# Ninth MLP tile: three groups of row blocks in seven half-size products instead of two, and w1's sums made two tiles sooner

## The chip, the cores and the metric

The kernel runs on one core of a Trainium2 chip. The metric is the device time of one execution in microseconds (us). Before the change three runs gave 312.92 us (median), 311.91 us and 319.43 us; the execution that was profiled took 311.71 us.

TensorE (PE in the profile) multiplies, with its weight loads on a row of their own (PEld). VectorE (DVE), ScalarE (ACT) and GpSimd (POOL) do the element-wise work, and SyncE (SP) issues transfers. Each engine runs its own instructions in the order in which they stand, and waits where an operand that another engine makes is not ready, or where a buffer that it writes is still being read.

## The reference

Attention with decays for 8 batches, 8 heads, 576 positions and head size 64 gives `x`, of 8 x 576 rows with 512 columns. A low-rank mixer over the positions follows, and then an MLP with a first layer `w_ch1` (512 to 2048) and a second layer `w_ch2` (2048 to 512):

```python
xt = x.transpose(0, 2, 1)
h = xt @ U @ V
u = x + h.transpose(0, 2, 1)
ch = np.maximum(u @ w_ch1, 0.0) @ w_ch2
return (u + ch).astype(np.float32)
```

## The kernel before, in words

The 4608 rows of `u` are cut into nine MLP tiles of 512 rows, `j` = 0 to 8; the text counts them from one, so that the ninth tile is `j` = 8. `u` transposed lies in `uT_t`. While tile `j` is in the MLP, the attention of batch `j + 1` is woven into it; batch 7, the last, belongs to the seventh tile (`j` = 6). The eighth and ninth tiles have no attention beside them and are written out in `last_tiles`.

**First layer of a tile.** Its 2048 outputs are 16 row blocks of 128. A plain block ("M" in the lists below, `unit(n)` for n below 16) is four matmuls of 128x512 into one PSUM bank, then a relu on ACT into `y1_t` (`y_t` in the profile). The blocks come in the order 0, 8, 1, 9, 2, 10 and so on. Group g is blocks 2g, 2g + 1, 8 + 2g and 9 + 2g, that is, four blocks: group 0 is M 0 to M 3, and group 3 is M 12 to M 15.

**A group in seven products.** Instead of four plain blocks, a group can be computed by Winograd's form of Strassen's product: seven products of half the rows, half the depth and half the blocks, of four matmuls of 128x256 each. The text writes "7/0" for product 7 of group 0. `seventh(n, g)` does this, with three PSUM banks for a group:

- bank a, from the pool `ps_mm` of three banks: 1, then 6, 7 and 4 are added to it in turn. After 1, 6 and 7 ACT copies the bank to an SBUF buffer `kept` (the rows `COPY q_all<-ps_y`), and the next of the chain may write only once the copy has read. After 4 ACT writes the relu.
- bank c, from the pool `one`: 5, and later 3.
- bank d: half of a tile of two banks from the pool `two`, taken once for each MLP tile; group g takes half g % 2.

After 2, after the later of 5 and 7, and after 3, DVE adds a copy to a bank and takes the maximum with zero (`finish`: a TENSOR_TENSOR `y_t<-ps_y,q_all` and a TENSOR_SCALAR `y_t<-y_t`). The copies lie in `shares[g % 2]`, the two query buffers `q_all0` and `q_all1`. `sum_up(a, z)` then makes two sums of a group's outputs for the second layer on DVE (`y_sums`).

The products need sums of quarters of `w1` (`sum_of_w1`, four tiles in the freed key and value buffers: `w1_sums` is `k_all2`, `v_all2`, `k_all0`, `v_all0`) and of the tile's `uT_t` (`sum_of_u`, four in `v_all1` for the eighth tile and `k_all1` for the ninth). Both are made on DVE.

**Second layer.** In the tiles from the third on it is also seven products, each of two units of 16 matmuls of 128x256 (units 16 to 29; `NF` is 16), on banks a, b and c of `ps_mm`. DVE drains them (`o_sb<-ps_y,o_sb`), POOL adds `u` to three of the partial results (`o_sb<-o_sb,u_t`), and SP stores.

**Order.** Everything is emitted in one program order, which each engine keeps. In tiles two to seven a list of steps with a place (a unit's number, fractions too) is merged with the units; in `last_tiles` the order was written out in loops. Before the change both last tiles take groups 1 and 2 in seven products and groups 0 and 3 in plain blocks, and the sums of `w1`, over blocks 2 to 5 of each half (1024 elements a row of a partition), are made at the start of the eighth tile, between that tile's sums of `u`.

Of the kernel before, what the change touches and what calls it, by code (L numbers as in the profile page):

```python
# [67 lines left out]
def kernel(  # L68
# [18 lines left out]
    B, H, S, D = q.shape  # L87
# [8 lines left out]
    NF = dff // P  # L96
# [5 lines left out]
    NT = B * S // 512  # L102
# [191 lines left out]
    def scale_head(b, h):  # L294

        x = v_sets[b % NSET][:, :, h, :]
        act.activation(out=x, in_=x, func=AF.Copy, scale=vs64[:, h:h + 1])


    def clear_pads(b):  # L300
        m, pad = (NB - 1, slice(HALF, P)) if b % 2 == 0 else (0, slice(0, HALF))
        for x in (k_sets, v_sets):
            pool.memset(x[b % NSET][pad, m, :, :], 0.0)

    def load_for_turns(b):

        for c in range(0, NB, 2):
            pair = range(c, min(c + 2, NB))
            load_q(b, pair)
            for m in pair:  # L310
                load_block(k_sets[b % NSET], k, b, m)
        for m in range(NB):
            load_block(v_sets[b % NSET], v, b, m)
# [13 lines left out]
    def wait_for_turns(b):  # L327

        wanted = [ch % NRING for ch in range(4 * b, 4 * b + 4)]
        for a, n in turns_of(b):  # L330
            if any(ch in wanted for ch in range(a, a + n)):
                pool.tensor_copy(out=landed[:, 0:n], in_=ring["uT"][:, a:a + n, 0, 0])
# [250 lines left out]
    def attention_steps(b, at, gap, at_mixer, at_turn=2):  # L583

        x_t = work.tile([P, NB, dm], BF16, tag="x_t", name="x_t")
        sts = [{} for _ in range(NHP)]
        mst = {}
        steps = []

        for hp in range(NHP):  # L590
            if b < NRUNS:
                steps.append((at[hp] - (3 if hp else 1), 4, lambda hp=hp: scale_v(b, hp)))
            steps.append((at[hp], 1, lambda hp=hp: att_transposes(b, hp, sts[hp])))
            steps.append((at[hp] + gap, 2, lambda hp=hp: visit(b, hp, sts, x_t)))
        steps.append((at[NHP], 0, lambda: visit(b, NHP, sts, x_t)))
        steps.append((at_mixer, 0, lambda: mix_middle(b, x_t, mst)))
        steps.append((at_mixer + 2, 0, lambda: mix_up_full(b, x_t, mst)))
        part = (NB - 1) * (1 - b % 2)
        steps.append((at_mixer + (2.5 if b % 2 else 5 if b > 2 else 8), 0, lambda: (
            mix_up(b, part, x_t, mst))))  # L600
        for i, (a, n) in enumerate(turns_of(b)):
            steps.append((at_mixer + 3.2 + i, 1, lambda a=a, n=n: mix_turn_by_dma(a, n)))
        if NTURN <= b + 1 < B:
            for i, (src, dst, c) in enumerate(
                    (src, dst, c) for c in range(0, NB, 2)
                    for src, dst in ((in_blocks(q_raw[(b + 1) % NQ]), qT_sets[(b + 1 - NTURN) % 2]),
                                     (k_sets[(b + 1) % NSET], kT_sets[(b + 1 - NTURN) % 2]))):
                steps.append((at_turn + i, 5, lambda src=src, dst=dst, c=c: (
                    turn_by_dma(src, dst, c))))
        steps.sort(key=lambda s: s[:2])  # L610
        return steps
# [324 lines left out]
    def w1_quarter(i, c):  # L936
        return w1_sb[:, 2 * c:2 * c + 2, i * HF * P:(i + 1) * HF * P]

    def sum_of_w1(n, a, z):

        f = slice(a * P, z * P)
        (a11, a12), (a21, a22) = ([w1_quarter(i, c)[:, :, f] for c in range(2)] for i in range(2))
        s1, s2, s3, s4 = (x[:, :, f] for x in w1_sums)
        to, x, y, op = (
            (s1, a21, a22, ALU.add), (s2, s1, a11, ALU.subtract),
            (s3, a11, a21, ALU.subtract), (s4, a12, s2, ALU.subtract),
        )[n]
        dve.tensor_tensor(out=to, in0=x, in1=y, op=op)

    def sums_of_w2(part):  # L950

        f = slice(part * HF // 2, (part + 1) * HF // 2)
        (b11, b12), (b21, b22) = (
            [w2_sb[:, fh * HF:(fh + 1) * HF, q * HD:(q + 1) * HD][:, f, :] for q in range(2)]
            for fh in range(2)
        )
        t3, t2, t4 = (w2_sums[:, i, f, :] for i in range(3))
        for to, x, y, op in (
            (t3, b22, b12, ALU.subtract), (t2, t3, b11, ALU.add), (t4, b21, t2, ALU.subtract),
        ):  # L960
            dve.tensor_tensor(out=to, in0=x, in1=y, op=op)

    def last_sum_of_w2(part):
        f = slice(part * HF // 2, (part + 1) * HF // 2)
        x = w2_sb[:, 0:HF, HD:dm][:, f, :]
        dve.tensor_tensor(out=x, in0=x, in1=w2_sb[:, 0:HF, 0:HD][:, f, :], op=ALU.subtract)
# [406 lines left out]
    n = 16  # L1373
# [79 lines left out]
            tc.tile_pool(name="ps_" + name, bufs=n, space=bass.MemoryType.PSUM))  # L1453


    def last_tiles():

        tiles = [mlp_units(j) for j in (NT - 2, NT - 1)]
        for i in range(4):
            steps = [lambda: tiles[0][1]["sum_of_u"](i), lambda: sum_of_w1(i, 2, 6)]  # L1460
            for step in steps if i < 2 else steps[::-1]:
                step()
        for units, steps in tiles:
            seventh, sum_up = steps["seventh"], steps["sum_up"]
            for n in range(3):
                units[n]()
            seventh(1, 1)
            units[3]()
            for n, g in ((6, 1), (2, 1), (5, 1), (7, 1)):
                seventh(n, g)  # L1470
            sum_up(0, 2)
            for n, g in ((1, 2), (2, 2), (4, 1), (6, 2), (5, 2), (3, 1), (7, 2)):
                seventh(n, g)
            sum_up(2, 4)
            for n, x in zip(range(12, NF), (4, 3, None, None)):
                units[n]()
                if x:
                    seventh(x, 2)
                if x == 3:
                    sum_up(4, 6)  # L1480
            for n in range(NF, NF + 14):
                units[n]()
                if n == NF + 11 and steps is tiles[0][1]:
                    for i in range(4):
                        tiles[1][1]["sum_of_u"](i)

    for j in range(1, NT - 2):
        if j == 1:
            clear_pads(4)
        steps = []  # L1490
        if j == 1:
            steps = sorted(
                attention_steps(2, (5, 8.5, 12, 15.5, 21), 1.5, 22, 8) + late
                + [(at, 3, lambda i=i: sums_of_w2(i)) for i, at in enumerate((3.2, 21.5))],
                key=lambda s: s[:2]
            )
        elif j + 1 < B:
            last = 17 if j < 5 else 16
            steps = attention_steps(j + 1, (-1.5, 2.5, 6.5, 10.5, last), 1.5, last + 1.8)
        if j == 2:  # L1500
            steps += [(at, 3, lambda i=i: last_sum_of_w2(i)) for i, at in enumerate((2, 3))]
        if 1 < j and j + 2 < B:
            wait_for_turns(j)
            load_for_turns(j + 2)
            if j + 3 < B:
                clear_pads(j + 3)
        if j + 2 < B:
            at = 22 if j == 1 else 20
            steps += [(at + h, 4, lambda h=h: scale_head(j + 2, h)) for h in range(H)]
        steps.sort(key=lambda s: s[:2])  # L1510
        for n, unit in enumerate(units1 if j == 1 else mlp_units(j)[0]):
            while steps and steps[0][0] <= n:
                steps.pop(0)[2]()
            if j > 1 or n >= 3:
                unit()
        for s in steps:
            s[2]()
    last_tiles()


# [29 lines left out]
```

## Time and profile before

| | |
|---|---|
| median of three runs | 312.92 us (311.91 to 319.43) |
| the profiled execution | 311.71 us |
| its span, first to last instruction | 310.0 us |
| PE busy | 302.9 us, 98% of the span |
| DVE busy | 244.7 us, 79% |
| ACT busy | 165.9 us, 54% |
| POOL busy | 131.8 us, 43% |
| granted TensorE clock | 1.00 throughout |
| eighth tile's first layer begins on PE at | 255.76 us |
| ninth tile's first layer begins on PE at | 281.05 us |
| ninth tile's second layer begins on PE at | 294.10 us |

Times within the span are counted from the span's start. A row of the timeline gives start, length, engine, operation, the tile written and those read, the shape, the count, and in brackets how long the engine was idle before and who ended that. A row with a count above one runs together instructions that follow each other. The length of such a row reaches a little into the next row, since instructions overlap; the distance between starts is what an instruction takes of its engine.

### The profile page before, as it was taken

How to read it: one execution, taken by the hardware profiler on the slowest of the kernel's cores; microseconds unless marked ns; L12 is line 12 of the kernel's file. 1: busy time of each engine (PE TensorE's matmuls, PEld its weight loads, DVE VectorE, ACT ScalarE, POOL GpSimd, SP SyncE). 2: the span in 40 equal slices, each digit the busy share in tenths (PEclk: the TensorE clock that was granted, in tenths of full speed). 3: DMA queues.
4: the chain of work that ended last, by engine and by line, in shares of the span. 5: the costliest groups of instructions: out<-in, count | busy, mean ns of one | idle time of the engine just before them, and what ended most of it. 6: DMA issues, size and time to landing. Idle time of an engine off the chain costs nothing.

```text
span 310.0 us, 9604 instructions
## 1 busy us (share of the span) xinstructions
PE 302.9 (98%) x4000; PEld 193.8 (63%) x4000; DVE 244.7 (79%) x598; ACT 165.9 (54%) x346; POOL 131.8 (43%) x172
## 2 busy tenths in 40 slices
PE   8899999999999999999999999999999999999995
PEld 3664446645544557845784578457855786686684
DVE  6867818878988997899689968996789788954954
ACT  8657605357625774567447844674377506504610
POOL 8592249649302952495158615940300030040040
PEclk9999999999999999999999999999999999999999
DMA  7999999999995999799999999999920043003003
GB/s 119 198 198 200 204 208 158 174 166 140 159 154 144 154 148 136 102 182 157 141 162 182 132 129 152 194 149 134 183 69 4 3 92 128 2 29 109 0 2 136
DMA packets 154523, 40.58 MB, mean 131 GB/s; under 512 B 139088, under 2 KB 153456, under 8 KB 154480
## 3 DMA queue, kind: packets, MB, share of 16 engines
q0 software_dynamic: 91344, 17.09, 72.2%
q1 hardware_dynamic: 63136, 22.88, 42.2%
q8 instruction: 31, 0.51, 0.7%
q14 instruction: 12, 0.10, 0.1%
HBM read 36.85 MB, written 9.44 MB: 149 GB/s over the span
## 4 chain that ended last, share of the span: by engine, by line
PE 85%; DMA 6%; DVE 5%; issue 1%; POOL 1%; SPq 0%; DVEq 0%
PE ps_y L25 70%; PE xh L25 5%; PE ps_b L25 4%; DMA kv_runs<-in_k_dram 2%; DMA kv_runs<-in_v_dram 2%; DMA y_sums<-in_k_dram 2%; PE sc L25 2%; PE ps_h L25 1%; PE pss L25 1%; DVE v_all L25 1%; PE ps_at L25 1%; DVE V_sb L25 1%; PE psq L25 0%; DVE qT_all L25 0%; DVE q_all L25 0%
## 5 line engine op out<-in xcount | busy, mean ns | idle before, releaser
L25 PE MATMUL ps_y<-uT_t,w_sb 128*128 128x512 bf16 (+1 forms) x544 | 121.6, 373 | 0.1
L25 ACT ACTIVATE y_t<-ps_y 128x512 bf16<-128x512 f32 x132 | 78.4, 597 | 57.4 <-PE ps_y L25 55.7
L25 PEld LDWEIGHTS <-w_sb 128*128 128x128 bf16 x560 | 52.9, 98 | 53.7 <-issue 0.4
L25 POOL TENSOR_TENSOR o_sb<-o_sb,u_t 128x512 f32<-128x512 f32 x21 | 23.9, 1151 | 106.5 <-DVE o_sb L25 99.2
L25 PEld LDWEIGHTS <-y_t 128*128 128x128 bf16 x576 | 55.1, 98 | 18.9
L25 PE MATMUL ps_y<-w_sb,y_t 128*128 128x256 bf16 (+1 forms) x352 | 57.5, 312 | 0.0
L25 DVE SCALAR_TENSOR_TENSOR S<-S,keep,pss 128x64 bf16<-128x64 bf16 x168 | 47.0, 280 | 5.1
L25 DVE TENSOR_TENSOR o_sb<-ps_y,o_sb 128x512 f32<-128x512 f32 (+1 forms) x37 | 24.4, 662 | 25.4 <-PE ps_y L25 11.7
L25 DVE TENSOR_TENSOR ret<-sc,qsrow 128x640 bf16<-128x640 f32 x48 | 39.3, 819 | 2.8 <-PE sc L25 2.7
L25 PEld LDWEIGHTS <-y_sums 128*128 128x128 bf16 x336 | 32.0, 98 | 5.0 <-issue 0.3
L25 POOL DMA_DIRECT2D k_all<-in_k_dram x36 | 30.1, 852 | 8.5 <-DMA w_sb<-in_moe_w_ch_dram 7.8
L25 ACT ACTIVATE v_all<-v_all,vs 128x320 bf16<-128x320 bf16 x40 | 18.7, 548 | 24.0 <-DMA v_all<-in_v_dram 17.0
L25 POOL DMA_DIRECT2D q_all<-in_q_dram x37 | 29.4, 802 | 4.8 <-DMA w_sb<-in_moe_w_ch_dram 3.9
L25 POOL DMA_DIRECT2D v_all<-in_v_dram x31 | 26.4, 882 | 7.2 <-DMA q_all<-in_q_dram 2.2
L25 PE MATMUL ps_y<-w_sb,y_sums 128*128 128x256 bf16 x224 | 27.4, 273 | 0.0
L25 PE MATMUL ps_y<-kv_runs,y_t 128*128 128x256 bf16 x224 | 26.9, 273 | 0.0
L25 ACT ACTIVATE x_t<-xh,xs 128x320 bf16<-128x320 f32 x48 | 22.7, 523 | 7.2 <-PE xh L25 5.5
L25 DVE TENSOR_TENSOR u_t<-ps_h,x_t 128x512 bf16<-128x512 f32 (+2 forms) x39 | 22.3, 628 | 2.5 <-PE ps_h L25 2.3
L25 PEld LDWEIGHTS <-k_all 64*64 64x64 bf16 (+2 forms) x596 | 12.8, 109 | 3.2 <-issue 2.1
L25 PE MATMUL ps_y<-kv_runs,y_sums 128*128 128x256 bf16 x112 | 14.1, 273 | 0.1
L25 PEld LDWEIGHTS <-ret 128*128 128x128 bf16 (+1 forms) x320 | 11.7, 98 | 2.4 <-issue 0.2
L25 POOL COPY landed<-uT_t 128x2 bf16<-128x2 bf16 (+1 forms) x6 | 1.1, 186 | 28.2 <-DMA uT_t<-u_t 28.2
(152 smaller groups left out, 337.2 us busy)
## 6 DMA issues: line engine op xcount, KB each, us to landing
out_dram<-o_sb SPq DMA_DIRECT2D x35, 256.0 KB, 3.1
w_sb<-in_moe_w_ch_dram POOLq DMA_DIRECT2D x8, 512.0 KB, 12.1
v_all<-in_v_dram POOLq DMA_DIRECT2D x25, 128.0 KB, 12.1
k_all<-in_k_dram POOLq DMA_DIRECT2D x24, 128.0 KB, 7.3
q_all<-in_q_dram POOLq DMA_DIRECT2D x20, 128.0 KB, 6.2
q_all<-in_q_dram POOLq DMA_DIRECT2D x12, 144.0 KB, 6.0
given<-in_v_dram SPq DMA_DIRECT2D x8, 128.0 KB, 5.1
kv_runs<-in_v_dram SPq DMA_DIRECT2D x3, 256.0 KB, 5.6
```

The lines of the kernel that those rows point to most:

```text
L25: return self._tc.keep_in_program_order(call(*args, **kwargs))
```

## The change

Three things change.

1. The ninth tile takes groups 0, 1 and 2 in seven products, and only group 3 (M 12 to M 15) in plain blocks. The order of the first layer is now a text: `THREE` for the ninth tile, `TWO` for the eighth, where `TWO` is the order as it was. "S g" is `sum_up` of group g.
2. The sums of `w1` take in block 0 and 1 of each half too (1536 elements instead of 1024). The first two are emitted in the sixth tile, the other two in the seventh, each time before unit 17.
3. The sums of `u` for the eighth tile are emitted in the seventh, before unit 28, that is, ahead of the drain of that tile's last product instead of behind it.

```diff
+    THREE = """
+        1 0; 1 1; 2 0; 6 0; 2 1; 7 0; 1 2; 5 0; 6 1; 2 2; 4 0; 3 0; 7 1; 6 2; 5 1; M 12; 7 2;
+        S 0; 3 1; 4 1; 5 2; 4 2; S 1; M 13; 3 2; S 2; M 14; M 15
+    """
+    TWO = """
+        M 0; M 1; M 2; 1 1; M 3; 6 1; 2 1; 5 1; 7 1; S 0; 1 2; 2 2; 4 1; 6 2; 5 2; 3 1; 7 2; S 1;
+        M 12; 4 2; M 13; 3 2; S 2; M 14; M 15
+    """
+    ends = [mlp_units(j) for j in (NT - 2, NT - 1)]
 ...
-        for i in range(4):
-            steps = [lambda: tiles[0][1]["sum_of_u"](i), lambda: sum_of_w1(i, 2, 6)]
-            for step in steps if i < 2 else steps[::-1]:
-                step()
 ...
+        for (units, steps), order in zip(ends, (TWO, THREE)):
+            for word in order.split(";"):
+                op, *args = word.split()
+                if op == "M":
+                    units[int(args[0])]()
+                elif op == "S":
+                    g = 2 * int(args[0])
+                    steps["sum_up"](g, g + 2)
+                else:
+                    steps["seventh"](int(op), int(args[0]))
 ...
+        if j in (NT - 4, NT - 3):
+            steps += [(16.2, 9, lambda i=i: sum_of_w1(i, 0, 6)) for i in (
+                (0, 1) if j == NT - 4 else (2, 3))]
+        if j == NT - 3:
+            steps += [(NF + 12, 9, lambda i=i: ends[0][1]["sum_of_u"](i)) for i in range(4)]
```

The first place is TensorE near the start of the ninth tile. Numbers behind the names tell buffers apart; what a row waits for stands in brackets, with "Activation" for ACT. Before the change, behind three plain blocks, stand product 1/1 (bank `ps_y1_5624`) and the fourth plain block:

```order
L25 LDWEIGHTS w1_sb_109
L25 MATMUL ps_y1_5624<-uT_t_112,w1_sb_109 128x256 [waits Activation_49]
L25 LDWEIGHTS w1_sb_109
L25 MATMUL ps_y1_5624<-uT_t_112,w1_sb_109 128x256
L25 LDWEIGHTS w1_sb_109
L25 MATMUL ps_y1_5624<-uT_t_112,w1_sb_109 128x256
L25 LDWEIGHTS w1_sb_109
L25 MATMUL ps_y1_5624<-uT_t_112,w1_sb_109 128x256
L25 LDWEIGHTS w1_sb_109
L25 MATMUL ps_y1_5630<-uT_t_112,w1_sb_109 128x512 [waits Activation_49]
```

After the change 1/0, 1/1 and 2/0 open the tile, and the rows below are the last matmul of 6/0 (bank a, `ps_y1_5605`), the four of 2/1 (`ps_y1_5617`, the tile that 2/0 has written too) and the first of 7/0 (bank a again):

```order
L25 MATMUL ps_y1_5605<-k_all1_75,v_all2_79 128x256
L25 LDWEIGHTS w1_sb_109
L25 MATMUL ps_y1_5617<-uT_t_112,w1_sb_109 128x256 [waits DVE_49]
L25 LDWEIGHTS w1_sb_109
L25 MATMUL ps_y1_5617<-uT_t_112,w1_sb_109 128x256
L25 LDWEIGHTS w1_sb_109
L25 MATMUL ps_y1_5617<-uT_t_112,w1_sb_109 128x256
L25 LDWEIGHTS w1_sb_109
L25 MATMUL ps_y1_5617<-uT_t_112,w1_sb_109 128x256
L25 LDWEIGHTS k_all0_74
L25 MATMUL ps_y1_5605<-k_all1_75,k_all0_74 128x256 [waits Activation_49]
```

What moved: half-size products stand where plain blocks stood, 2/1 waits for DVE, and only 2/1 lies between two writers of bank a.

The second place is VectorE at the start of the eighth tile's first layer (the `uT_t` rows are its sums of `u`, the `w_sb` rows the sums of `w1`, `o_sb<-ps_y_5225` the drain of the seventh tile's last product, and `y_t<-ps_y` the eighth tile's first `finish`); a piece of the difference:

```order
+L25 TENSOR_TENSOR o_sb<-ps_y_5179,o_sb 128x512
 L25 TENSOR_TENSOR v_all_78<-uT_t 128x2x2x128
-L25 TENSOR_TENSOR k_all_76<-w_sb 128x2x512
 L25 TENSOR_TENSOR v_all_78<-uT_t,v_all_78 128x2x2x128
-L25 TENSOR_TENSOR v_all_79<-k_all_76,w_sb 128x2x512
-L25 TENSOR_TENSOR k_all_74<-w_sb 128x2x512
 L25 TENSOR_TENSOR v_all_78<-uT_t 128x2x2x128
-L25 TENSOR_TENSOR v_all_77<-w_sb,v_all_79 128x2x512
 L25 TENSOR_TENSOR v_all_78<-uT_t,v_all_78 128x2x2x128
+L25 TENSOR_TENSOR o_sb<-ps_y_5225,o_sb 128x512
```

The four sums of `w1` have left this place, and the drain now stands behind the sums of `u`.

The third place is VectorE in the seventh tile's second layer after the change (`y_t<-y_t` are differences that the second layer needs, `o_sb<-ps_y` the drain of its second product, `u_t<-ps_h` the mixer's result for batch 7):

```order
L25 TENSOR_TENSOR y_t<-y_t 128x4x256 x2
L25 TENSOR_TENSOR k_all_74<-w_sb 128x2x768
L25 TENSOR_TENSOR v_all_77<-w_sb,v_all_79 128x2x768
L25 TENSOR_TENSOR o_sb<-ps_y_5179,o_sb 128x512
L25 TENSOR_TENSOR u_t<-ps_h_5202,x_t 128x4x128 x2
```

The two `w_sb` rows are new here; the rows around them stood next to each other before.

More of the change, by code (lines that the diff above doesn't have):

```diff
@@ L1453 @@
             tc.tile_pool(name="ps_" + name, bufs=n, space=bass.MemoryType.PSUM))
-    def last_tiles():
-        tiles = [mlp_units(j) for j in (NT - 2, NT - 1)]
-        for i in range(4):
-            steps = [lambda: tiles[0][1]["sum_of_u"](i), lambda: sum_of_w1(i, 2, 6)]
-            for step in steps if i < 2 else steps[::-1]:
-                step()
[L1463 to L1480, printed above, removed]
+    THREE = """
[7 more added lines that the diff above has]
+    ends = [mlp_units(j) for j in (NT - 2, NT - 1)]
+    def last_tiles():
+        for (units, steps), order in zip(ends, (TWO, THREE)):
[8 more added lines that the diff above has]
+                    steps["seventh"](int(op), int(args[0]))
             for n in range(NF, NF + 14):
                 units[n]()
-                if n == NF + 11 and steps is tiles[0][1]:
+                if n == NF + 11 and steps is ends[0][1]:
                     for i in range(4):
-                        tiles[1][1]["sum_of_u"](i)
+                        ends[1][1]["sum_of_u"](i)
     for j in range(1, NT - 2):
```

## The prediction

> **What bounds the kernel now.** I read the page's busy table first, then the chain that ended last, then the timeline of each engine in the last two tiles.
>
> ```profile
> PE 302.9 (98%) x4000; PEld 193.8 (63%) x4000; DVE 244.7 (79%) x598; ACT 165.9 (54%) x346; POOL 131.8 (43%) x172
> ```
>
> TensorE is busy for 98% of the span. The end of the chain, in order of time (start, length, what), says the same of the part that changes:
>
> ```profile
> 248.07 58.44 PE ps_y L25 x472
> 306.50 0.02 issue
> 306.53 0.42 DVE o_sb L25
> ```
>
> From 248.07 us to 306.50 the chain is TensorE alone, one matmul behind the other. What shortens TensorE's work there shortens the kernel; a change on DVE, ACT or POOL counts only if it makes TensorE wait. So the question is what TensorE gains in the ninth tile, and whether it then still never waits. TensorE's rows of that tile before the change:
>
> ```profile
> 281.05 4.05 PE L25 MATMUL ps_y<-uT_t,w_sb 128*128 128x512 bf16 x20
> 284.96 0.60 PE L25 MATMUL ps_y<-k_all,v_all 128*128 128x256 bf16 x4
> 285.39 0.60 PE L25 MATMUL ps_y<-uT_t,w_sb 128*128 128x256 bf16 x4
> 285.83 1.04 PE L25 MATMUL ps_y<-k_all,k_all 128*128 128x256 bf16 x8
> 286.70 1.04 PE L25 MATMUL ps_y<-uT_t,w_sb 128*128 128x256 bf16 x8
> 287.58 0.60 PE L25 MATMUL ps_y<-k_all,w_sb 128*128 128x256 bf16 x4
> ...
> 292.37 1.89 PE L25 MATMUL ps_y<-uT_t,w_sb 128*128 128x512 bf16 x8
> 294.10 1.91 PE L25 MATMUL ps_y<-w_sb,y_t 128*128 128x256 bf16 x16
> 295.85 1.91 PE L25 MATMUL ps_y<-kv_runs,y_sums 128*128 128x256 bf16 x16
> ```
>
> The row of 281.05 is M 0 to M 2, 1/1 and M 3; then come 6/1 (284.96), 2/1 (285.39), 5/1 and 7/1 (285.83), 1/2 and 2/2 (286.70) and 4/1. The starts follow each other without a gap.
>
> **The change part by part. (1) Fewer columns on TensorE.** Group 0 was four plain blocks and becomes seven products. The last two blocks take 294.10 - 292.37 = 1.73 us, so 0.865 for one and 3.46 for four. Six products lie between 284.96 and 287.58, 0.437 each, so 3.06 for seven. TensorE's work shrinks by 3.46 - 3.06 = 0.40 us. That is all that this change can win. The bounds are narrow, since both forms stand in the tile many times; from the row of 281.05, 284.96 - 281.05 - 0.437 = 3.47 for the four blocks, 0.41.
>
> **(2) New waits at the tile's start.** Here the rows of ACT and DVE count (ACT's copies to `kept`, DVE's first `finish`):
>
> ```profile
> 284.33 0.58 ACT L25 COPY q_all<-ps_y 128x512 f32<-128x512 f32 x1
> 285.14 0.60 ACT L25 ACTIVATE y_t<-ps_y 128x512 bf16<-128x512 f32 x1 [0.23 <-PE ps_y L25]
> 285.63 0.58 ACT L25 COPY q_all<-ps_y 128x512 f32<-128x512 f32 x1
> ...
> 281.63 0.68 DVE L25 TENSOR_TENSOR o_sb<-ps_y,o_sb 128x512 f32<-128x512 f32 x1
> 286.10 0.69 DVE L25 TENSOR_TENSOR y_t<-ps_y,q_all 128x512 bf16<-128x512 f32 x1 [3.79 <-PE ps_y L25]
> 286.83 0.29 DVE L25 TENSOR_SCALAR y_t<-y_t 128x512 bf16<-128x512 bf16 x1
> ```
>
> Bank a: 6/1 starts on TensorE at 284.96, its copy at 285.63 and ends at 286.21, and 7/1 starts at 286.27 (one product after 285.83). The chain is 1.25 us and a handover. Before, three products' time lay between two writers of bank a (1.31 us), which just covers it. After, 1/0 and 6/0 are three apart, but 6/0 and 7/0 only two (0.87). Alone, that would hold TensorE for 1.25 + 0.04 - 0.87 = 0.42 us (the handover of 0.04 is taken from the end of part 4).
>
> Bank d: 2/1 (285.39) was read by DVE from 286.10 to 286.79, that is, until 1.40 us after its start, and 2/2 came four products behind it, 1.75 us, so it found the read ended. After, 2/0 and 2/1 are two products apart, and the order shows that 2/1 waits for DVE although it writes the other half: both halves are one tile, and the wait goes by the tile. 2/0 would start at 281.05 + 2 x 0.437 = 281.92. DVE is free by then (its drain ends at 282.31), and 1/0's copy ends at 281.05 + 1.25 = 282.30, so the read runs from 282.63 to 283.32. 2/1 has its turn at 281.05 + 4 x 0.437 = 282.80 and starts at 283.36: **TensorE waits 0.56 us**. 7/0 then has its turn at 283.80. Its copy (6/0 at 282.36, plus 1.25) ends at 283.61, so the wait on bank a is covered by that on bank d. The two don't add up; the longer one counts.
>
> Further on I followed the list with these numbers. 2/2 stands five products behind 2/1 (2.18 us against 1.44). 3/0, 3/1 and 3/2 each come four products' time (1.75) behind 5 of their group. M 12 to M 15 take banks whose relu has ended. 1/2, 6/2 and 7/2 overwrite copies that group 0's `finish` has read by then, the tightest being 6/2: its copy is due at about 287.96, and 3/0's add has read at 287.87. No further wait comes out.
>
> Sum of 1 and 2: -0.40 + 0.56 = **+0.16 us**. The ends: -0.40 with no wait, and +0.58 if a second wait of the bank a kind (0.42) shows further on.
>
> **(3) w1's sums in the sixth and seventh tiles.** At the eighth tile's start a sum over 1024 elements took DVE 0.60 us of its time, one over 512 took 0.33:
>
> ```profile
> 256.98 0.68 DVE L25 TENSOR_TENSOR k_all<-w_sb 128x1024 bf16<-128x1024 bf16 x1
> 257.58 0.42 DVE L25 TENSOR_TENSOR v_all<-uT_t,v_all 128x512 bf16<-128x512 bf16 x1
> 257.91 0.68 DVE L25 TENSOR_TENSOR v_all<-k_all,w_sb 128x1024 bf16<-128x1024 bf16 x1
> ```
>
> So one over 1536 should take 0.87, and two 1.74. They stand ahead of the drain of the second layer's second product, where DVE was idle (the first two rows are of the sixth tile, the next two of the seventh):
>
> ```profile
> 211.94 1.28 DVE L25 TENSOR_TENSOR y_t<-y_t 128x1024 bf16<-128x1024 bf16 x2
> 215.46 0.69 DVE L25 TENSOR_TENSOR o_sb<-ps_y,o_sb 128x512 f32<-128x512 f32 x1 [2.23 <-ACT at_diag L25]
> 243.37 1.28 DVE L25 TENSOR_TENSOR y_t<-y_t 128x1024 bf16<-128x1024 bf16 x2
> 246.63 0.69 DVE L25 TENSOR_TENSOR o_sb<-ps_y,o_sb 128x512 f32<-128x512 f32 x1 [1.98 <-ACT at_diag L25]
> 248.78 1.91 PE L25 MATMUL ps_y<-kv_runs,y_t 128*128 128x256 bf16 x16
> ```
>
> The idle time is 2.23 and 1.98 us, so 1.74 fits with 0.24 to spare in the tighter one. If that cover is gone, the drain of 246.63 comes late, and behind it the mixer's adds; the first that TensorE needs of it is the bank for 248.78, 1.46 us after the drain's end at 247.32. Cost: nothing, up to two sums of 1.7 us each.
>
> The eighth tile loses four sums (2.4 us of DVE). TensorE did not wait there, so nothing is won.
>
> **(4) The sums of u ahead of a drain.** In the seventh tile the drain of the last product ran at 256.04; now four sums stand ahead of it, from 254.28 + 0.60 on, 1.4 us:
>
> ```profile
> 250.47 3.90 SPq L25 DMA_TRANSPOSE uT_t<-u_t  x3
> 254.28 0.69 DVE L25 TENSOR_TENSOR o_sb<-ps_y,o_sb 128x512 f32<-128x512 f32 x1 [0.34 <-issue]
> 255.76 4.05 PE L25 MATMUL ps_y<-uT_t,w_sb 128*128 128x512 bf16 x20
> 256.04 0.69 DVE L25 TENSOR_TENSOR o_sb<-ps_y,o_sb 128x512 f32<-128x512 f32 x1 [1.07 <-PE ps_y L25]
> ```
>
> The drain then ends at about 256.97 instead of 256.73, and its bank is wanted by the third block at 255.76 + 2 x 0.865 = 257.49. The sums need the transposed chunk issued at 250.47. Of such transfers the view of transfers says (count, median us to landing):
>
> ```profile
> uT_t<-u_t SPq DMA_TRANSPOSE x15, 2.8
> ```
>
> So it lands at 253.3, ahead of the sums. Cost: nothing. Were it to land only when TensorE reads it, at 255.76, the drain would end at 257.84 and the third block wait 0.4 us.
>
> The end of the ninth tile's first layer has one more thing to cover:
>
> ```profile
> 294.30 0.60 ACT L25 ACTIVATE y_t<-ps_y 128x512 bf16<-128x512 f32 x1 [0.27 <-PE ps_y L25]
> 294.93 0.43 DVE L25 TENSOR_TENSOR y_sums<-y_t 128x512 bf16<-128x512 bf16 x1 [0.17 <-ACT y_t L25]
> 295.39 0.42 DVE L25 TENSOR_TENSOR y_sums<-y_sums,y_t 128x512 bf16<-128x512 bf16 x1
> ```
>
> The last sum ends at 295.81, and the second product starts at 295.85: a handover of 0.04 or less, with no slack. Nine `finish` pairs of 0.93 (0.73 to the second instruction, 0.20 behind it) and three pairs of sums of 0.79 are 10.7 us of DVE between 282.63 and M 15's relu, which ends at about 295.06: 12.4 us of room. Followed in order, group 2's sums end 0.4 us ahead of it. So DVE holds nothing up, but not by much.
>
> **Level.** 311.71 + 0.16 = 311.87 for an execution like the profiled one. That stands below the median shown, 312.92; the third run is 311.91. I put the forecast on the mean of the three that agree, (311.71 + 311.91 + 312.92) / 3 = 312.18, so 312.3.
>
> **The rivals.** *A, the wait is smaller or absent.* If 2/1 does not wait by the tile, 7/0 still waits 0.42 and the sum is 0.0; with no wait at all -0.40, 311.8 on the same level. For it: the halves are different banks. Against it: the order names DVE. *B, DVE becomes the bound in the ninth tile (slower).* The first two `finish` pairs before stood 1.42 apart, since the second waited for a copy (287.52 against 286.10):
>
> ```profile
> 287.52 0.69 DVE L25 TENSOR_TENSOR y_t<-ps_y,q_all 128x512 bf16<-128x512 f32 x1 [0.40 <-ACT q_all L25]
> ```
>
> If all nine did, they and the sums would take 15.2 us instead of 12.4, and the second layer's second product would start 2.7 us late: 315.0. It decides from 0.4 us of delay on. Against it: later pairs ran 0.93 apart once DVE had a queue. *C, a half-size product does not cost half.* The page has for weight loads (count, busy us, mean ns):
>
> ```profile
> L25 PEld LDWEIGHTS <-w_sb 128*128 128x128 bf16 x560 | 52.9, 98 | 53.7 <-issue 0.4
> ```
>
> If each of the 28 loads of 98 ns showed between matmuls of 128x256, the tile would take 2.7 us more: 312.18 - 0.40 + 2.7 = 314.5. The starts above, 0.437 / 4 = 0.109 per matmul, speak against it.
>
> The Trainium skill, TensorE: Matmul & The Clock Gate, "Back-to-back issue gap", gives about 131 ns a matmul at 512 columns and 81 at 128 for a stream of weight loads and matmuls; an estimate between them of 98 at 256 would make seven products (28 x 98 = 2.7 us) dearer than four blocks (16 x 131 = 2.1), and the change a loss of 0.6 us. This trace disagrees: 865 / 4 = 216 ns at 512 columns, and 109 at 256.
>
> **How the numbers follow.** Forecast (one wait of about half a microsecond, all else hidden) 0.65; A 0.15; B 0.12; C 0.02; another cause 0.06. The range reaches down to A's end on the level of the fastest run, 311.71 - 0.40, less the 0.2 between the two fastest: 311.1. It reaches up to the slowest of the three, 312.92 + 0.16, and half of B's delay, 1.35: 314.4. Two per cent is 6.3 us, about what a measurement of this kernel can tell from no change; no term comes near it. Faster by that 0.01, within 0.96, slower 0.03.
>
> **What would show it.** TensorE's row at the ninth tile's start breaks at about 283.3, named after DVE's `y_t`, for 0.5 to 0.6 us, and nowhere else; the second layer starts at 294.2 to 294.3. In the sixth and seventh tiles two rows `128x1536` of 0.95 us stand in DVE's idle time. The forecast is wrong if TensorE waits twice, if the drain near 246.6 moves by over 1.5 us, or if `y_sums` is late at 295.9.

## The result, and the profile after

The changed kernel took 313.81 us (median of 22 runs, 311.84 to 315.18). The kernel before, run beside it, took 312.35 us (22 runs, 311.32 to 319.43). The ratio is 1.004, with a 95% interval of 1.002 to 1.0059: slower by 0.4%, far inside two per cent, and more than the 0.16 us that the sum gave. The profiled execution took 313.54 us, with a span of 311.5 us (before 311.71 and 310.0).

The first view is the page's busy table, the second the end of the chain in order of time:

```profile
PE 302.4 (97%) x3997; PEld 195.5 (63%) x4012; DVE 248.7 (80%) x604; ACT 165.9 (53%) x346; POOL 131.8 (42%) x172
```

```profile
249.21 34.63 PE ps_y L25 x284
284.67 23.28 PE ps_y L25 x196
```

The chain is still TensorE alone, but it now has a seam, at 284.67. TensorE's timeline of the changed ninth tile shows what stands there (the first row is the eighth tile's start):

```profile
257.07 4.05 PE L25 MATMUL ps_y<-uT_t,w_sb 128*128 128x512 bf16 x20
...
270.12 1.91 PE L25 MATMUL ps_y<-w_sb,y_t 128*128 128x256 bf16 x16
...
282.35 1.47 PE L25 MATMUL ps_y<-uT_t,w_sb 128*128 128x256 bf16 x12
283.66 0.60 PE L25 MATMUL ps_y<-k_all,v_all 128*128 128x256 bf16 x4
284.67 0.60 PE L25 MATMUL ps_y<-uT_t,w_sb 128*128 128x256 bf16 x4 [0.42 <-DVE y_t L25]
285.11 0.60 PE L25 MATMUL ps_y<-k_all,k_all 128*128 128x256 bf16 x4
...
293.82 1.89 PE L25 MATMUL ps_y<-uT_t,w_sb 128*128 128x512 bf16 x8
295.55 1.91 PE L25 MATMUL ps_y<-w_sb,y_t 128*128 128x256 bf16 x16
297.29 1.91 PE L25 MATMUL ps_y<-kv_runs,y_sums 128*128 128x256 bf16 x16
```

Product 2/1 had its turn at 283.66 + 0.437 = 284.10 and began at 284.67: a wait of 0.57 us, named after DVE's `y_t`. The bracket says 0.42, since the modelled end of the row ahead reaches into the gap; the distance of the starts is the measure. No other row of the tile breaks off. The first layer takes 295.55 - 282.35 = 13.20 us, before 294.10 - 281.05 = 13.05: **+0.15**. The eighth tile's first layer takes 270.12 - 257.07 = 13.05.

DVE's timeline answers for the three places where instructions were added (sixth tile, seventh tile, the drain behind the sums of `u`) and for the end of the ninth tile's first layer:

```profile
213.50 1.28 DVE L25 TENSOR_TENSOR y_t<-y_t 128x1024 bf16<-128x1024 bf16 x2
214.71 0.95 DVE L25 TENSOR_TENSOR k_all<-w_sb 128x1536 bf16<-128x1536 bf16 x1
215.69 0.96 DVE L25 TENSOR_TENSOR v_all<-k_all,w_sb 128x1536 bf16<-128x1536 bf16 x1
216.76 0.69 DVE L25 TENSOR_TENSOR o_sb<-ps_y,o_sb 128x512 f32<-128x512 f32 x1
...
244.67 1.29 DVE L25 TENSOR_TENSOR y_t<-y_t 128x1024 bf16<-128x1024 bf16 x2
245.87 0.95 DVE L25 TENSOR_TENSOR k_all<-w_sb 128x1536 bf16<-128x1536 bf16 x1
246.74 0.95 DVE L25 TENSOR_TENSOR v_all<-w_sb,v_all 128x1536 bf16<-128x1536 bf16 x1
247.93 0.69 DVE L25 TENSOR_TENSOR o_sb<-ps_y,o_sb 128x512 f32<-128x512 f32 x1 [0.24 <-issue]
...
257.31 0.41 DVE L25 TENSOR_TENSOR v_all<-uT_t,v_all 128x512 bf16<-128x512 bf16 x1
257.65 0.68 DVE L25 TENSOR_TENSOR o_sb<-ps_y,o_sb 128x512 f32<-128x512 f32 x1
...
283.93 0.69 DVE L25 TENSOR_TENSOR y_t<-ps_y,q_all 128x512 bf16<-128x512 f32 x1 [0.32 <-PE ps_y L25]
...
295.62 0.42 DVE L25 TENSOR_TENSOR y_sums<-y_sums,y_t 128x512 bf16<-128x512 bf16 x1
296.38 0.42 DVE L25 TENSOR_TENSOR y_sums<-y_t 128x512 bf16<-128x512 bf16 x1 [0.33 <-ACT y_t L25]
```

In the seventh tile the drain follows the differences by 247.93 - 244.67 = 3.26 us, as before (246.63 - 243.37), and in the sixth by 3.26 us too (before 215.46 - 211.94 = 3.52): the sums lie in what was idle time. The read that 2/1 waits for runs from 283.93 to 284.62.

So the changed instructions account for 0.15 us. The rest lies elsewhere. The eighth tile begins 257.07 - 255.76 = 1.31 us later than in the profile of before, and nearly all of that comes before the sixth tile, in instructions that the change does not touch. And the time less the span is 2.04 us, where it was 1.71: 0.33 us that no row shows. 1.31 + 0.15 + 0.33 = 1.79 of the 1.83 us between the two profiled executions. What the experiments had to settle is which of this belongs to the kernel.

The first piece of the 1.31 us is seen on ACT near 100 us. ACT scales the values of a coming batch there (`v_all`), head by head, as soon as their transfer has landed. First before, then after:

```profile
93.59 3.27 ACT L25 ACTIVATE v_all<-v_all,vs 128x320 bf16<-128x320 bf16 x7 [3.02 <-DMA v_all<-in_v_dram]
```

```profile
96.91 3.27 ACT L25 ACTIVATE v_all<-v_all,vs 128x320 bf16<-128x320 bf16 x7 [6.10 <-DMA v_all<-in_v_dram]
100.20 0.58 ACT L25 COPY uT_t<-ps_ut 128x512 bf16<-128x512 bf16 x1
...
100.84 0.35 PE L25 MATMUL sc<-qT_all,kT_all 64*64 64x64 bf16 x19 [0.64 <-ACT uT_t L25]
```

The values landed 3.3 us later in the second execution (GpSimd had issued the five loads 0.95 us later, from 76.12 instead of 75.17; the other 2.4 us passed between issue and landing). ACT stood still for them, and the copy `uT_t<-ps_ut` behind them in ACT's queue held TensorE for 0.64 us.

### The profile page after: what moved, and what is told of

The parts are those of the page before. It is cut to its first block, busy times and chain, and to the rows that moved or that the text cites. A ratio compares the mean times of both kernels' runs of the same rounds, so it can differ in the third digit from the quotient of the medians.

```text
span 311.5 us, 9630 instructions
## 1 busy us (share of the span) xinstructions
PE 302.4 (97%) x3997; PEld 195.5 (63%) x4012; DVE 248.7 (80%) x604; ACT 165.9 (53%) x346; POOL 131.8 (42%) x172
## 4 chain that ended last, share of the span: by engine, by line
PE 83%; DVE 6%; DMA 4%; SPq 3%; issue 2%; ACT 1%; POOL 0%; DVEq 0%; POOLq 0%; ACTq 0%
PE ps_y L25 69%; PE xh L25 5%; PE ps_b L25 4%; SPq L25 3%; DMA given<-in_v_dram 2%; DMA kv_runs<-in_v_dram 2%; PE sc L25 2%; PE pss L25 1%; PE ps_h L25 1%; PE ps_at L25 1%; DVE v_all L25 1%; DVE S L25 1%; DVE V_sb L25 1%; DVE qT_all L25 1%; PE psq L25 0%
## 5 line engine op out<-in xcount | busy, mean ns | idle before, releaser
L25 PE MATMUL ps_y<-uT_t,w_sb 128*128 128x512 bf16 (+1 forms) x536 | 119.2, 371 | 0.6 <-DVE y_t L25 0.4
L25 ACT ACTIVATE y_t<-ps_y 128x512 bf16<-128x512 f32 x129 | 76.6, 597 | 46.8 <-PE ps_y L25 45.6
L25 PE MATMUL ps_y<-w_sb,y_t 128*128 128x256 bf16 (+1 forms) x345 | 56.4, 310 | 0.5 <-issue 0.2
L25 PEld LDWEIGHTS <-k_all 64*64 64x64 bf16 (+2 forms) x604 | 13.9, 109 | 4.9 <-issue 2.8
L25 ACT COPY q_all<-ps_y 128x512 f32<-128x512 f32 x15 | 8.4, 586 | 13.3 <-PE ps_y L25 13.0
L25 DVE TENSOR_TENSOR y_t<-ps_y,q_all 128x512 bf16<-128x512 f32 x15 | 10.3, 686 | 5.4 <-ACT y_t L25 3.8
```

Of the source, the lines that this page charges most:

```text
L25: return self._tc.keep_in_program_order(call(*args, **kwargs))
```

## The experiments

The theory (T1 below): the terms of the prediction are right, and what exceeds them is scatter ahead of the ninth tile, from values that land late. The rivals: the moved sums of `w1` cost it (T2), or the wait in the ninth tile is longer in other executions than in the profiled one (T3).

**The changed kernel again, and the kernel before beside it as a control.** No edit.

> The changed kernel once more, unaltered, for a second trace and more times. Theory T1 (the ninth tile costs 0.15 us net, and the other 1 us or so arises in the first 110 us, where batch 3's values land late in some executions and ACT's queue holds TensorE): 0.8 to 1.6 us over the kernel before, ninth tile's first layer 13.2 us on TensorE with one wait of 0.57, and the second trace again differs from before ahead of 110 us. Theory T2 (the moved sums of w1 cost it): the difference shows in the sixth or seventh tile. Theory T3 (the wait in the ninth tile is longer in some executions): the first layer of the ninth tile is longer than 13.2 us.

> The kernel before, unaltered, as a control: within 0.3 us of the kernel before under every theory, and a second trace of it that shows how far the start of the program (the first 110 us) differs between two executions of one program. T1 expects it to differ by up to 1 us there; if it doesn't, T1's late landing belongs to the changed program.

Measured: changed 312.96 us (311.94 to 314.04, 12 runs), ratio 0.9999 (0.9974 to 1.0025) against 312.85 us of before; the control 312.68 us (311.16 to 316.2), ratio 0.9985 (0.9963 to 1.0008). The changed ninth tile took 296.03 - 282.83 = 13.20 us again, so T3 falls. The 0.4% did not show in this comparison. T1 had expected 0.8 to 1.6 us over the kernel before, which is a miss. But this profile too lost time ahead of the ninth tile, in another place:

```profile
161.60 3.74 ACT L25 ACTIVATE v_all<-v_all,vs 128x320 bf16<-128x320 bf16 x8 [8.16 <-DMA v_all<-in_v_dram]
...
165.61 2.18 DVE L25 SCALAR_TENSOR_TENSOR S<-S,keep,pss 128x64 bf16<-128x64 bf16 x7 [1.43 <-ACT S L25]
...
166.13 1.02 PE L25 MATMUL ps_y<-uT_t,w_sb 128*128 128x512 bf16 x4 [0.24 <-ACT y_t L25]
```

It is the same mechanism at the end of the fourth tile: ACT waits for values, and the relu that TensorE needs stands behind them, as does ACT's cast of `S`, for which DVE waits 1.43 us. From the plain blocks at 163.13 to the next `pss` at 167.85 TensorE takes 4.72 us, where the profile of before has 166.21 - 162.50 = 3.71. The place differs from execution to execution.

**The moved sums alone.** The ninth tile keeps two groups; parts 2 and 3 of the change stay.

```diff
-        for (units, steps), order in zip(ends, (TWO, THREE)):
+        for (units, steps), order in zip(ends, (TWO, TWO)):
```

> Parts 2 and 3 of the change without part 1: both last tiles take two groups in seven products, while the sums of w1 stay in the sixth and seventh tiles over 1536 elements. T1: 0 to 0.3 us over the kernel before if the late landing is chance, 0.7 to 1.3 over it if any change of the program brings it. T2: 0.8 to 1.3 us over, shown in the sixth or seventh tile. T3: as the kernel before. TensorE in the ninth tile's first layer: 13.05 us.

Measured: 312.58 us (311.58 to 316.74), ratio 1.0006 (0.9982 to 1.003); ninth tile 294.87 - 281.81 = 13.06 us. The moved sums cost nothing that this can tell, and between batch 2 and batch 7 the profile loses 0.20 us (in the table below), where T2 needs 0.8 or more in the sixth or seventh tile. T2 falls.

**An order without the wait.** The same 21 products and 4 plain blocks, in an order in which no product writes a tile or a bank that is still being read: two or three products stand between any two writers of bank a in group 0, three between 2/0 and 2/2, and four between 2/2 and 2/1.

```diff
     THREE = """
-        1 0; 1 1; 2 0; 6 0; 2 1; 7 0; 1 2; 5 0; 6 1; 2 2; 4 0; 3 0; 7 1; 6 2; 5 1; M 12; 7 2;
-        S 0; 3 1; 4 1; 5 2; 4 2; S 1; M 13; 3 2; S 2; M 14; M 15
+        1 0; 1 1; 2 0; 6 0; 1 2; 5 1; 2 2; 7 0; 5 0; 6 1; 4 0; 2 1; 3 0; 7 1; S 0; 6 2; M 12;
+        5 2; 7 2; 3 1; S 1; M 13; 4 1; 3 2; 4 2; S 2; M 14; M 15
```

> The changed kernel with its ninth tile's list in another order, so that products of bank a lie at least three products apart, 2/0, 2/2 and 2/1 four or more, and 3 five behind the later of 5 and 7. All three groups stay in seven products. T1: the ninth tile's first layer takes 12.65 us on TensorE without a wait, 0.55 less than the changed kernel; the time lies 0.55 below e1_after_again, which may still be above the kernel before by 0.3 to 1. T2: the same difference to e1. T3: 1 us or more below e1, and 0.4 below the kernel before.

TensorE's timeline, first the start of the tile, then its end:

```profile
281.72 1.47 PE L25 MATMUL ps_y<-uT_t,w_sb 128*128 128x256 bf16 x12
283.03 0.60 PE L25 MATMUL ps_y<-k_all,v_all 128*128 128x256 bf16 x4
283.47 0.60 PE L25 MATMUL ps_y<-uT_t,w_sb 128*128 128x256 bf16 x4
283.90 0.60 PE L25 MATMUL ps_y<-k_all,k_all 128*128 128x256 bf16 x4
...
294.34 0.93 PE L25 MATMUL ps_y<-w_sb,y_t 128*128 128x256 bf16 x7
```

No row breaks off, and the first layer takes 294.34 - 281.72 = 12.62 us: 0.43 less than before, 0.58 less than with the change. That is the gain of part 1 by itself and the price of the wait by itself. The time was 312.46 us (310.85 to 315.85), ratio 0.9989 (0.9967 to 1.0012). Repeated:

> The order without a wait in the ninth tile, a second time: 0.43 us less in the ninth tile than before, ratio 0.9987 with an interval of about 0.002 to either side.

It came to 312.46 us again (311.01 to 316.33), ratio 0.9997 (0.9972 to 1.0022), ninth tile 294.58 - 281.96 = 12.62. The gain is plain in the rows, and too small for either comparison of whole executions. In both, this order's median lies below the changed kernel's, by 0.50 and 0.43 us.

**Two halves of one tile, or two tiles.** Product 2/0 gets a tile of its own, so that 2/1 shares none with it.

```diff
+            elif n == 2 and g == 0:
+                held["L", g, "d"] = banks["one"].tile(
+                    [P, 2, 2 * P], FP32, tag="att", name="ps_y1")
             elif n == 2:
```

> As the change, but product 2/0 writes a tile of its own in the pool one, so that 2/1 no longer shares a tile with it. If the wait goes by the tile, 2/1 does not wait any more, and the wait on bank a that it covered shows instead: 7/0 waits 0.42 us for ACT's copy of 6/0, and the ninth tile's first layer takes 13.05 - 0.40 + 0.42 = 13.07 us, 0.13 less than with the change. If the wait on y_t had another reason (DVE late), it stays: 13.20. If the two waits added up, it would drop by the whole 0.58, to 12.62.

The profiled execution is a long one (316.44 us; in the second tile it is behind the changed kernel's profiles by 3.6 us or more already), so it is read for its ninth tile alone:

```profile
285.40 1.47 PE L25 MATMUL ps_y<-uT_t,w_sb 128*128 128x256 bf16 x12
286.71 0.60 PE L25 MATMUL ps_y<-k_all,v_all 128*128 128x256 bf16 x4
287.15 0.60 PE L25 MATMUL ps_y<-uT_t,w_sb 128*128 128x256 bf16 x4
288.03 0.60 PE L25 MATMUL ps_y<-k_all,k_all 128*128 128x256 bf16 x4 [0.28 <-DVE y_t L25]
...
298.47 1.80 PE L25 MATMUL ps_y<-w_sb,y_t 128*128 128x256 bf16 x15
```

2/1 (287.15) follows 6/0 by 0.44 and does not wait any more. 7/0 had its turn at 287.59 and began at 288.03: 0.44 us, where 0.42 was expected. The first layer takes 13.07 us, the number expected. The bracket names DVE's `y_t`, whose TENSOR_SCALAR ends at about the same time, but 7/0 writes bank a, and in the order of the changed kernel it waits for ACT alone. What it needs is ACT's copy of 6/0, whose row stands at 287.39 for 0.59 us, that is, until 287.98:

```profile
287.39 0.59 ACT L25 COPY q_all<-ps_y 128x512 f32<-128x512 f32 x1 [0.28 <-ACT q_all L25]
```

So both waits are there in the changed kernel, one covers the other, and the wait on bank d goes by the tile. Time 313.13 us (311.3 to 317.52), ratio 1.0006 (0.9978 to 1.0034).

**THREE alone, with the sums where they were.** The four sums of `w1`, over six blocks of each half, go back to the eighth tile's start, and the sums of `u` with them.

```diff
     def last_tiles():
 
+        for i in range(4):
+            both = [lambda: ends[0][1]["sum_of_u"](i), lambda: sum_of_w1(i, 0, 6)]
+            for step in both if i < 2 else both[::-1]:
+                step()
...
-        if j in (NT - 4, NT - 3):
-            steps += [(16.2, 9, lambda i=i: sum_of_w1(i, 0, 6)) for i in (
-                (0, 1) if j == NT - 4 else (2, 3))]
-        if j == NT - 3:
-            steps += [(NF + 12, 9, lambda i=i: ends[0][1]["sum_of_u"](i)) for i in range(4)]
```

> The list THREE alone: w1's sums, over the six blocks, are made at the eighth tile's start as before, and so are the sums of u. Ninth tile 13.20 us with one wait of 0.6 on y_t, as with the change. Eighth tile: four sums of 0.95 instead of 0.68 end some 1.1 us later than before; 13.05 us if the products that need them still find them, up to 14.2 if not. Time less span: 2.0 to 2.1 us if the 0.33 us outside the span go with the list THREE, 1.7 if they go with the changed program as a whole.

TensorE's eighth tile, and the start and end of its ninth:

```profile
256.67 4.05 PE L25 MATMUL ps_y<-uT_t,w_sb 128*128 128x512 bf16 x20
...
262.33 0.60 PE L25 MATMUL ps_y<-uT_t,w_sb 128*128 128x256 bf16 x4
263.10 0.60 PE L25 MATMUL ps_y<-uT_t,w_sb 128*128 128x256 bf16 x4 [0.17 <-DVE y_t L25]
...
270.05 1.15 PE L25 MATMUL ps_y<-w_sb,y_t 128*128 128x256 bf16 x9
...
282.28 1.47 PE L25 MATMUL ps_y<-uT_t,w_sb 128*128 128x256 bf16 x12
...
295.48 1.91 PE L25 MATMUL ps_y<-w_sb,y_t 128*128 128x256 bf16 x16
```

The eighth tile's first layer takes 13.38 us, 0.33 more than with the change. 2/2 (263.10) begins 0.77 us after 1/2 (262.33), not 0.44: it writes the tile that 2/1 has written, and DVE, busy with sums until then, reads 2/1 only from 262.36 to 263.05. That is what parts 2 and 3 are worth once the sums span six blocks. The ninth tile again takes 13.20. Time 314.15 us (312.15 to 317.99), ratio 1.0032 (1.0006 to 1.0059). The time less the span is 1.79 us on the mean (expected 2.0 to 2.1, or 1.7), so most of the extra outside the span does not go with the list THREE.

**Without the loads of the values.** From the changed kernel, the kernel before and the order without a wait, the loads of the values of batches 3 to 7 are left out, 25 transfers; ACT scales stale values in their place, so these batches' attention is not that of the reference.

```diff
-        for m in range(NB):
-            load_block(v_sets[b % NSET], v, b, m)
```

> The changed kernel without the loads of the values of batches 3 to 7 (25 transfers; ACT scales what an earlier batch left, so that the attention of these batches computes something else). T1, the scatter ahead of the ninth tile comes from values that land late and hold ACT: no v_all row of ACT ends an idle time named after that transfer any more, the eighth tile begins within 0.3 us of the same kernel built from before, the times of the runs lie within about 1 us, and the median stands 0.15 (ninth tile) + 0.33 (outside the span) = 0.5 us above that kernel. T4, the scatter has another source (stores, the transposes, the loads of q and k): the times still lie 2 to 4 us apart, and the two kernels differ by any amount up to 1.5 us.

> The kernel before without the same 25 loads: the base for the run above. T1: 310.5 to 312.0 us, times within about 1 us of each other, ninth tile's first layer 13.05 us. T4: scatter as in the full kernel, 311.2 to 315.5.

> The order without a wait in the ninth tile, without the same 25 loads. T1: 0.43 us below the kernel before without them (12.62 against 13.05 in the ninth tile), with an interval that leaves no difference out, and 0.9 us below the changed kernel without them. T4: not to be told from either.

Measured: changed 312.6 us (311.33 to 314.62), before 311.79 us (310.38 to 315.39), order without a wait 312.2 us (310.76 to 316.02); against the full kernel before the ratios are 0.9996 (0.9974 to 1.0018), 0.9961 (0.9933 to 0.9988) and 0.9972 (0.9947 to 0.9997). The first two medians lie 0.81 us apart, where 0.5 was expected. One part of T1 held, and one fell. What held shows in the busy time of each engine between 90 and 250 us. The columns are the stretch, its length, then the busy time of PE, PEld, DVE, ACT and POOL with their counts, the granted clock, the DMA share (the time that packets took; it can exceed 1) and GB/s. The fences are before, after, and after without these loads:

```profile
90.00:250.00 160.00, 159.90 (x2328) 101.72 (x2327) 135.40 (x304) 96.68 (x209) 70.67 (x87) 1.00 1.33 133
```

```profile
90.00:250.00 160.00, 158.94 (x2311) 100.94 (x2316) 137.94 (x306) 96.67 (x209) 69.44 (x86) 1.00 1.35 134
```

```profile
90.00:250.00 160.00, 160.00 (x2344) 101.58 (x2344) 139.16 (x308) 97.15 (x210) 53.22 (x66) 1.00 0.98 115
```

Without the loads TensorE is busy for the whole 160.00 us, in all three kernels; with them it was busy for 158.94 to 159.90. A finer measure is the distance between starts, from the mixer's product `ps_at` of batch 2 to that of batch 7:

| profile | `ps_at` of batch 2 at | to that of batch 7 | more than 155.06 |
|---|---|---|---|
| changed, without the loads | 89.93 | 155.06 | 0 |
| before, without the loads | 91.8 | 155.05 | 0 |
| no wait, without the loads | 90.99 | 155.22 | 0.16 |
| before | 88.9 | 155.32 | 0.26 |
| before, control | 89.53 | 155.06 | 0 |
| sums alone | 89.73 | 155.26 | 0.20 |
| no wait, first and second | 89.84, 89.21 | 155.06, 155.93 | 0, 0.87 |
| THREE alone | 89.44 | 155.69 | 0.63 |
| halves apart | 93.06 | 155.52 | 0.46 |
| changed, first, second, third | 89.14, 89.39, 89.46 | 156.38, 156.62, 156.33 | 1.32, 1.56, 1.27 |

What is lost between the second and the seventh tile thus goes with these loads. That ACT's wait for values is the path is shown by the rows of the first two profiles of the changed kernel, and not for the third. There the largest piece is a pause for which the view names no other engine and no transfer, and ACT does not wait for values at the time:

```profile
145.55 0.25 PE L25 MATMUL sc<-qz,kvT 64*64 64x64 bf16 x6 [0.77 <-issue]
```

What fell is that this is the scatter: without the loads the times still lie 3.3 to 5.3 us apart, where T1 had expected about 1 us. It arises in the opening too. In the column of the granted clock, the kernel before without the loads has in its opening

```profile
12.00:14.00 2.00, 0.63 (x20) 0.49 (x22) 1.22 (x3) 0.62 (x1) 0.26 (x1) 1.00 1.48 232
14.00:16.00 2.00, 1.42 (x40) 1.12 (x35) 0.00 (x0) 0.37 (x2) 2.00 (x4) 0.58 0.47 100
16.00:18.00 2.00, 2.00 (x38) 1.52 (x35) 1.83 (x4) 1.30 (x4) 2.00 (x4) 0.50 0.69 84
18.00:20.00 2.00, 1.94 (x16) 1.46 (x15) 1.59 (x3) 0.58 (x1) 2.00 (x3) 0.50 1.23 202
20.00:22.00 2.00, 2.00 (x41) 1.59 (x40) 0.35 (x2) 1.02 (x3) 2.00 (x4) 0.71 1.25 208
```

TensorE has little to do from 12 us on, and then runs at half its clock: by this column for 6.84 us in all (four times 1 less the clock, over the stretches of 2 us). This execution reaches batch 2's `ps_at` at 91.8. THREE alone had 0.50 from 16 to 18 us, and 3.44 us in all; the order without a wait had 3.40 us without these loads, and the halves apart 3.40. In the profile of before the clock was 1.00 in all of these stretches. The Trainium skill, TensorE: Matmul & The Clock Gate, "What's actually happening", describes a gate that halves the clock after an idle window of about 3.4 us and whose windows run free of the kernel; the value of 0.50, its changing place and lengths of once or twice 3.4 us agree with that. That such a window must be idle throughout is not what these rows show: in the 3.4 us ahead of the fall (10.92 to 14.33) TensorE was busy for 1.64. The order without a wait could not be told from the kernel before here (expected 0.43 us less, measured 0.4 more): a miss of the expectation. With times 5 us apart, a difference of this size does not show.

**The changed kernel a third time.**

> The changed kernel unaltered, a third time. If the 0.4% of the first comparison belongs to the kernel, the ratio is again about 1.004 and the median about 314. If only what the traces show in every execution belongs to it (0.15 us in the ninth tile, 0.33 outside the span), it is 0.48 us above the kernel before, a ratio of 1.0015, and the rest was the scatter of single executions.

Measured: 312.89 us (311.46 to 317.4), ratio 1.0014 (0.9984 to 1.0043) against 312.71 us of before, ninth tile 295.81 - 282.62 = 13.19. The three comparisons of the changed kernel give 1.004, 0.9999 and 1.0014. With the means of the compared runs (the control counted with the kernel before in the second), the differences are 1.10, 0.11 and 0.30 us; their mean is 0.50, and resampling the runs gives 0.15 to 0.86. What every profile of it shows is 0.15 us in the ninth tile and, on the mean of the runs, 2.08 - 1.71 = 0.37 outside the span: 0.52 us, a ratio of 1.0017.

## Why the prediction was right or wrong

The time lies within the range, and no rival came true. The forecast, though, added only 0.16 us to the kernel before, and the first comparison puts the difference at 0.6 to 1.8 us (1.002 to 1.0059). By its own steps:

**Part 1 was right.** The order without a wait measures the smaller work alone: -0.43 us, where the text had -0.40. By the estimate from the Trainium skill, TensorE: Matmul & The Clock Gate, "Back-to-back issue gap", it would have been a loss of 0.6; these rows disagree with it a second time.

**Part 2 was right**, in place, cause and size: one wait, at 2/1, named after DVE's `y_t`, 0.57 us (0.56). With 2/0 in a tile of its own the covered wait on bank a came out at 0.44 (0.42). That the two don't add up is shown, too, since removing the longer one won 0.13 us, and removing both won 0.58. No further wait appeared.

**Part 3 was right.** A sum took 0.87 us of DVE (245.87 to 246.74) and the seventh tile's drain did not move against its neighbours. The sixth tile's pair, where the second reads what the first wrote, is 0.98 apart; 2.23 us of idle time held it.

**Part 4 was right.** The drain ended at 258.33, and its bank was wanted at 257.07 + 1.73 = 258.80. At the end of the first layer DVE was ahead by 0.33 us (0.4 forecast).

**Rival B** fell short of its condition: DVE had the 0.33 us left. **Rival A** describes what happens when the tile is split, and gave 13.07, that is, +0.02 where the text had 0.0. **Rival C** is excluded by the distance of 0.437 us.

**The step that failed is the one headed Level**: "311.71 + 0.16 = 311.87 for an execution like the profiled one." It took two things for given. The first is that the time outside the span stays at 1.71 us. It was 2.02 to 2.12 in the 22 runs of the first comparison, and this alone is twice the sum. The second is that everything ahead of the ninth tile repeats to a tenth. It does not: from batch 2 to batch 7 the profiled executions lose 0 to 1.56 us, in part through ACT's wait for values, and they reach batch 2's `ps_at` at 88.90 to 89.84 us, the one long one at 93.06. The sum was right for the instructions that it counted, and it was a sum over a tile, not over an execution. The forecast of 312.3 lies 1.5 us below the median measured: 0.37 is the time outside the span, 0.17 the level itself (312.18 against 312.35 for the kernel before), and about 0.9 stands in none of the prediction's terms. The remark that two per cent is about what a measurement of this kernel can tell was wrong too: the intervals here reach 0.2 to 0.3% to either side.

How far the 0.4% belongs to the kernel stays open in part. 0.52 us is accounted for, and the mean of the three comparisons (0.50) needs no more. But all three profiles of the changed kernel lost 1.27 to 1.56 us between batch 2 and batch 7, while the seven others with these loads lost 0 to 0.87. The instructions in those tiles are the same, and the order without a wait, which has the same instructions up to the ninth tile and the same number in it, lost 0 and 0.87. Three executions cannot tell whether this is chance or belongs to the changed program. For the time outside the span there is a sign, and no proof of the cause. On the mean of the runs it was 1.71 for the kernel before, 1.70 for the sums alone, 1.77 and 1.79 for the order without a wait, 1.79 for THREE alone, 2.06 with the halves apart, and 2.08, 2.06 and 2.08 for the changed kernel: nearly the same in each run of a program, and different from program to program. In the profile of the changed kernel one more packet of 8 KB, of a queue that the page calls "instruction", starts 1.6 us after the span's end. The view of the transfers from 312 to 316 us has nothing else (packets, MB, share):

```profile
q14 instruction: 1, 0.01, 0.8%
```

All three profiles of the changed kernel have it, as have the halves apart and the changed kernel without the loads of the values (1.92 us outside the span); the eight other profiles, with means of 1.70 to 1.79, do not. No run changes this packet alone.

## What to carry to other kernels

When a plain block is split into smaller products that share banks, count the distance between writers in time, not in places: a read chain of 1.25 us was covered by three products of 0.437 and no longer by two, and an order that keeps that distance won the whole 0.43 us. A wait goes by the tile as it was allocated: two halves of a two-bank tile hold each other up, and a second wait may hide beneath the one that shows, so that taking one away (0.13 us) is worth less than taking both (0.58). And where a term is a few tenths of a microsecond in an execution of 310, the distance between starts in the trace settles it, while a comparison of whole executions, which here lie 2 us and more apart from fastest to slowest, does not.

## What was not expected of the hardware

Late transfers reach TensorE through an engine that itself is half idle: ACT (53% busy) waited up to 8.16 us for values, and a copy and relus behind them in its queue held TensorE for 0.64 and 0.24 us. The loads of the values raise the changed kernel's DMA share from 0.98 to 1.35 between 90 and 250 us, in which they landed up to 3.3 us apart from one execution to the next. The granted clock fell to 0.50 for about 3.4 or 6.8 us in the opening of four of the thirteen profiled executions, at different places. And the time outside the span, 2.06 to 2.08 us on the mean for the changed kernel, was 1.77 and 1.79 for the order without a wait, which differs from it in the rows of one tile; the longer time goes with one more instruction packet behind the span.
